# Sixteen score groups as float16 pairs with high halves cast on GpSimd, and five operand pairs and eleven stores issued later, in a fused attention and gated-layer kernel

## The chip, the cores and the metric

The program runs on one core of a Trainium2 chip, as one launch. The metric is the device time of that launch in microseconds. The kernel before took 1107.22 us (median of three runs, 1106.39 to 1107.66).

In what follows TensorE is PE (its weight loads are PEld), VectorE is DVE, ScalarE is ACT, GpSimd is POOL, and SyncE, which issues nearly all DMAs, is SP.

## The reference, cut to what matters

```python
def _attn_ref(q, k, v):                      # 8 batches, 12 heads, 448 positions, head size 64
    scores = (1 / sqrt(64)) * np.matmul(q, k.transpose(0, 1, 3, 2)) - np.log(448)
    attn = 1.0 / (1.0 + np.exp(-scores))     # a sigmoid, no softmax
    return np.matmul(attn, v)

def _moe_ref(x, w_gate, w_val, w_out):       # x: 3584 tokens x 768; hidden size 1536
    gate = 1.0 / (1.0 + np.exp(-(x @ w_gate)))
    val = x @ w_val
    return gate * val @ w_out
```

The attention output, with its heads side by side, is the `x` of the second function. The weights come as float64 and are turned into float32 on the chip.

## The kernel before, in words

**Two parts.** The first part computes the attention and, beside it, prepares operands. The second part computes the gated layer in visits: four pairs of batches, each visited twice for the first layer (`visits` of kind A, parts 0 and 1) and once for the output layer (kind C). A product of two matrices there is done with seven half-size products (Strassen's way, `N_OPS = 7`), each operand of which is a pair of float16 matrices, a high half and a low half. Every matmul of the second part has 128 x 128 weights and 448 columns.

**The attention loop.** It runs over 24 groups `m` (8 batches times 3 groups of four heads) and 7 blocks `g` of keys: 168 beats. In a beat PE computes the scores of `(m, g)` (`scores`, line 541), then the product with the values for the block two beats earlier (`values`, line 576); ACT turns the scores into sigmoids (line 568) and copies finished outputs (line 593). The scores come in two forms. In float32, PE issues 4 matmuls straight from the loaded queries and keys (`qk`). In the split form a group has been turned into float16 pairs beforehand, and PE issues 12 matmuls for a beat: low times high, high times low, high times high. `in_halves(m)` says which form a group has: the odd groups from 3 on, and the even ones listed in `ALSO` (line 37: 14, 18, 22), 14 groups in all. Beats of a group in float32 are called f32 beats below, the others f16 beats.

**How a group is split (`split_qk`, line 508).** It is a generator in three steps. Two groups ahead (at `g = 0` of `m - 2`), DVE takes the largest absolute value of each row (lines 514 and 516). At `g = 4` of `m - 2`, four tiny matmuls are queued behind the next beat's scores, which bring the largest of all rows to every row (`qk_sums`, line 559; ACT copies it out, line 570). One group ahead (at `g = 0` of `m - 1`), DVE makes a power of two from it (lines 522 and 523), casts the scaled group into the high half (line 527, twice 128 x 896), subtracts to get the low half (line 529, twice 128 x 896), and computes the factor that ACT undoes the scale with (lines 531 and 532). The halves of odd groups lie in tiles `hl`, those of even groups in the tiles `b0` and `b1`. The scores of `(m, 0)` need all of this.

**What else runs in the loop.** The weights are converted (`convert`), one step in some of the beats: ACT and DVE put float32 words together (lines 213, 214, 224, 227), POOL clamps (line 207), DVE adds (line 272), POOL casts high halves (`whl`, line 390), DVE subtracts low halves (line 242), SP stores them. No step is made in beats `g = 0, 1` when the next group is in halves. From `m = 8` on the first pair of batches is loaded back as `x` (`load_x`), summed on DVE (`subtract_x`, line 358), and split into its 21 operands (`split_x`, line 420): for each, POOL casts the high half (line 390) and, one step later, DVE subtracts the low half (line 401). A step is made at `g = 2` and `g = 5` from `m = 12` on, so all 24 steps fall into the loop. Each two operands share a tile `b`; SP stores it to `b_dram` (line 427) so that it can be loaded again for the second visit of that pair, much later. The eighteen source tiles take their names in turn from `SUMS` and from `xt0` to `xt5`; `xt` tiles live in the pool of the attention part alone, those of `SUMS` longer.

**The visits.** A `Visit` runs the seven products of a unit, two units interleaved, one product (9 matmuls) and one `tick` at a time. Its operands are `self.b`; the first visit's products take operands in the order 0, 1, 2, 4, 3, 5, 6 (`ORDER`). Weight operands come through a ring of 8 tiles `A` that SP fills in program order. In each of the first four visits the next pair's `x` is loaded, summed on POOL and split by ACT and DVE (from tick 29 or 33 on), and stored.

**What sets the order.** Each engine runs its own instructions in the order in which the code issues them, and waits at semaphores. A few instructions that stand first on an engine behind the change from the first part to the second are put further ahead, to where their inputs are ready. SP's DMAs are issued in program order.

Of the kernel before, what the change touches and what calls it, by code (L numbers as in the profile page):

```python
# [15 lines left out]
ALU = mybir.AluOpType  # L16
# [19 lines left out]

ALSO = 14, 18, 22

# [13 lines left out]
JPS_OF_PARTS = (range(0, 4), range(4, 6))  # L52
# [9 lines left out]
def sigmoid_attention_glu_kernel(ctx: ExitStack, tc: tile.TileContext, qk, v, wg, wv, wo, out):  # L62

    nc = tc.nc
# [7 lines left out]
    KC = KT // 2  # L72
# [5 lines left out]
    N_OPS = 7  # L78
# [267 lines left out]
    xs, bs, new_bs = {}, {}, {}  # L346
# [42 lines left out]
    def scaled_gpsimd(to, x, s):  # L389
        nc.gpsimd.tensor_scalar(out=to, in0=x, scalar1=s, scalar2=1.0, op0=ALU.mult, op1=ALU.mult)  # L390
# [20 lines left out]
    def load_b(pr):  # L411

        for at in range(KEPT + 1):
# [4 lines left out]
            yield  # L418

    def split_x(pr, cast=scaled, engine=nc.gpsimd):  # L420

# [3 lines left out]
        for at in range(len(work) + 3):  # L425
            while unsent:
                nc.sync.dma_start(**unsent.pop(0))
            if at == len(work) + 2:
                yield
                break  # L430
# [63 lines left out]
    with tc.manual_schedule(), tc.tile_pool(name="att", bufs=2) as att, tc.tile_pool(name="sc", bufs=2, space=PSUM) as scp, \  # L494
# [10 lines left out]
        def in_halves(m):  # L505
            return 1 < m < B * NQ and (m % 2 == 1 or m in ALSO)

        def split_qk(m):
# [17 lines left out]
            for t in range(2):  # L526
                nc.vector.tensor_scalar(out=hl[0][:, t], in0=x[:, :, t], scalar1=s_[:, t:t + 1], scalar2=None, op0=ALU.mult)
            for t in range(2):
# [111 lines left out]
        first_x = 2 * NQ + 2  # L640
        tags = itertools.chain(SUMS, (f"xt{i}" for i in range(2 * KC)))

# [8 lines left out]
        for m in range(B * NQ):  # L651
            for g in range(7):
# [11 lines left out]
                if g == (m == 2) and in_halves(m + 1):  # L664
                    next(splitting[m + 1])
                if g == (5 if m == 1 else 4) and in_halves(m + 2):
                    next(splitting[m + 2])
# [13 lines left out]
                if m >= first_x + 2 and g in (2, 6):  # L681
                    next(x_sums, None)
                if m >= first_x + 4 and g in (2, 5):
                    next(splits, None)
# [9 lines left out]
        assert next(x_loads, None) is None and next(x_sums, None) is None  # L694
        for _ in splits:
            pass

# [181 lines left out]
    class Visit:  # L879


        def __init__(self, v_):
            (_, self.pr, part), nxt = visits[v_], visits[v_ + 1]
            self.v_, self.jps, self.b, self.keep = v_, JPS_OF_PARTS[part], dict(new_bs), nxt[0] == "C"
            self.p, self.ticks = 0, starts[v_ + 1] - starts[v_]
# [10 lines left out]
        def tick(self):  # L896
            self.p += 1
            p, left = self.p, self.ticks - self.p
            if p % 2 == 0 and self.early:
                self.early.pop(0)()  # L900
# [242 lines left out]
```

## Time and profile before

| | |
|---|---|
| median of three runs | 1107.22 us |
| the profiled execution, its own time | 1107.39 us |
| span of its instructions | 1105.7 us |
| granted TensorE clock | 1.00 |
| matmuls and weight loads on PE | 7738 each |
| busy: PE / DVE / ACT / POOL, whole span | 1100.1 / 770.2 / 672.1 / 423.4 us |
| `bd<-b` stores of operand pairs | 30 of 448 KB, 3 of 224 KB |

Times in the profile are microseconds from the first instruction. A row of groups reads: line, engine, operation, what it writes `<-` what it reads, partitions x elements, count, then busy time and the mean of one in ns, then the idle time of the engine just before. A row of the timeline reads: start, length, engine, line, operation. Rows with the same engine may overlap, since an engine takes up the next instruction before the last one's end is recorded. The chain of waits is followed back from the last instruction: at each step to what released it.

### The profile page before, as it was taken

The page shows a single profiled execution, that of the slowest core. Times are in us where ns is not written, and L with a number is a line of the kernel's source. Part 1 is how long each engine was busy: PE and PEld are TensorE (multiplying, and loading weights), DVE is VectorE, ACT ScalarE, POOL GpSimd, SP SyncE. Part 2 cuts the span into 40 slices and gives each one's busy share as a digit, 9 for nine tenths or more (in the row PEclk, how much of TensorE's full clock was granted, in tenths as well). Part 3 has the DMA queues.
Part 4 walks back from the last instruction along what each step waited for, and adds up shares of the span by engine and source line. Part 5 has one row for each costly group of instructions (what it writes and reads, how often), then busy time and mean ns, then how long its engine had stood idle before and what let it go on. Part 6 is the DMA issues. An engine that isn't in the chain of part 4 may idle for free.

```text
span 1105.7 us, 21560 instructions
## 1 busy us (share of the span) xinstructions
PE 1100.1 (99%) x7738; PEld 556.9 (50%) x7738; DVE 770.2 (70%) x1303; ACT 672.1 (61%) x1273; POOL 423.4 (38%) x398
## 2 busy tenths in 40 slices
PE   9999999999999999999999999999999999999998
PEld 3444454455555555555555555555555555555554
DVE  4998999977964474555667766674349687776863
ACT  5888888877576675765566767665545253243330
POOL 1132232243731351432334433242365293672940
PEclk9999999999999999999999999999999999999999
DMA  8899888689898467733766899797856877868644
GB/s 320 275 297 349 282 276 284 233 269 366 268 304 279 152 216 219 258 105 93 225 204 203 267 360 302 216 313 199 241 155 198 262 217 216 274 201 247 187 124 142
DMA packets 174540, 265.35 MB, mean 240 GB/s; under 512 B 49249, under 2 KB 151265, under 8 KB 174433
## 3 DMA queue, kind: packets, MB, share of 16 engines
q1 hardware_dynamic: 174144, 263.60, 74.2%
q8 instruction: 60, 0.98, 0.4%
q14 instruction: 48, 0.39, 0.1%
q10 hardware_dynamic: 288, 0.38, 0.1%
HBM read 182.48 MB, written 81.43 MB: 239 GB/s over the span
## 4 chain that ended last, share of the span: by engine, by line
PE 99%; ACT 0%; DVE 0%; DVEq 0%; issue 0%
PE un L737 78%; PE av L583 12%; PE sc L553 10%; PE sc L618 0%; ACT a L568 0%; PE un L705 0%; DVE g L1023 0%; DVEq L1138 0%; PE sc L559 0%; PE sc L565 0%; DVE bias L85 0%; DVEq L1023 0%
## 5 line engine op out<-in xcount | busy, mean ns | idle before, releaser
L737 PEld LDWEIGHTS <-A 128*128 128x128 f16 x3024 | 295.5, 98 | 275.9 <-DMA ad<-whl 0.7
L737 PE MATMUL un<-b,A 128*128 128x448 f16 x1512 | 296.5, 352 | 0.0
L737 PE MATMUL un<-b,v 128*128 128x448 f16 x1512 | 296.4, 352 | 0.0
L737 PE MATMUL un<-hh,A 128*128 128x448 f16 x1008 | 272.9, 352 | 0.0
L737 PEld LDWEIGHTS <-v 128*128 128x128 f16 x1512 | 147.7, 98 | 137.5
L737 PE MATMUL un<-hl,A 128*128 128x448 f16 x504 | 177.6, 352 | 0.0
L583 PE MATMUL av<-a,v 64*64 64x448 f32 x1344 | 156.8, 538 | 0.0
L948 POOL TENSOR_TENSOR g<-c,g 128x448 f32<-128x448 f32 x44 | 59.7, 1357 | 173.9 <-DVE c L720 79.3
L207 POOL TENSOR_SCALAR wf<-wf 128x384 f32<-128x384 f32 x72 | 42.1, 585 | 203.2 <-ACT wf L230 120.4
L568 ACT ACTIVATE a<-sc,bias,qkb 128x896 f32<-128x896 f32 x98 | 108.1, 1104 | 12.7 <-PE sc L553 9.3
L720 DVE TENSOR_TENSOR c<-un,u 128x448 f32<-128x448 f32 x72 | 44.8, 623 | 94.5 <-PE un L737 84.0
L933 ACT ACTIVATE g<-c,back 128x448 f32<-128x448 f32 x72 | 48.1, 668 | 77.1 <-DVE c L720 76.4
L568 ACT ACTIVATE a<-sc,bias 128x896 f32<-128x896 f32 x70 | 70.4, 1007 | 30.0 <-PE sc L553 26.6
L358 POOL TENSOR_TENSOR v<-v 128x448 f32<-128x448 f32 x48 | 64.1, 1365 | 51.2 <-DVE hl L401 50.1
L358 POOL TENSOR_TENSOR b<-b 128x448 f32<-128x448 f32 x48 | 67.5, 1441 | 40.5 <-DVE hl L401 40.5
L583 PEld LDWEIGHTS av<-a,v 64*64 64x64 f32 x1344 | 49.3, 133 | 39.2 <-issue 29.6
L553 PE MATMUL sc<-qk 64*64 64x448 f32 x560 | 65.6, 540 | 0.4 <-ACT a L568 0.4
L753 ACT COPY p<-un 128x448 f32<-128x448 f32 x48 | 25.4, 528 | 58.4 <-PE un L737 58.3
L720 DVE TENSOR_TENSOR c<-un,p 128x448 f32<-128x448 f32 x48 | 29.8, 621 | 41.8 <-PE un L737 40.6
L553 PE MATMUL sc<-hl 64*64 64x448 f16 x924 | 57.5, 349 | 0.0
L358 POOL TENSOR_TENSOR r<-r 128x448 f32<-128x448 f32 x36 | 45.2, 1266 | 30.2 <-DVE b L401 29.9
L110 ACT ACTIVATE junk<-g 128x448 bf16<-128x448 f32 x88 | 50.5, 574 | 7.0 <-POOL g L948 6.0
(362 smaller groups left out, 1425.4 us busy)
## 6 DMA issues: line engine op xcount, KB each, us to landing
A<-ad SPq DMA_DIRECT2D x168, 192.0 KB, 3.3
A<-oo SPq DMA_DIRECT2D x168, 192.0 KB, 2.9
qk<-qk SPq DMA_DIRECT2D x23, 896.0 KB, 7.5
h<-g SPq DMA_DIRECT2D x88, 224.0 KB, 3.2
ad<-whl SPq DMA_DIRECT2D x84, 192.0 KB, 3.8
bd<-b SPq DMA_DIRECT2D x30, 448.0 KB, 3.4
b<-bd SPq DMA_DIRECT2D x30, 448.0 KB, 6.2
v<-vv SPq DMA_DIRECT2D x24, 448.0 KB, 4.9
```

The costliest lines, as they stand in the source:

```text
L110: nc.scalar.activation(junk[:, :x.shape[-1]], x, AF.Abs, accum_out=to)
L207: nc.gpsimd.tensor_scalar(out=f, in0=f, scalar1=F32_MAX, scalar2=F64_ZERO, op0=ALU.min, op1=ALU.max)
L358: engine.tensor_tensor(out=to, in0=x, in1=y, op=ALU.subtract)
L553: nc.tensor.matmul(sc[halves[p], h, :S], lhsT=ks_, rhs=qs, start=i == 0, stop=i == 2 or not in_halves(m))
L568: nc.scalar.activation(a, sc[:, :, :S], AF.Sigmoid, bias=bias, scale=unit)
L583: nc.tensor.matmul(avs[m][p][halves[h], :S], lhsT=vt[halves[p], g, h], rhs=a[halves[p], h], start=g == 0, stop=g == 6)
L720: engine.tensor_tensor(out=to, in0=x, in1=y, op=ALU.add)
L737: nc.tensor.matmul(acc, lhsT=w, rhs=m, start=begin and i == 0, stop=i == len(terms) - 1, skip_group_check=not begin)
L753: nc.scalar.copy(c, acc)
L933: nc.scalar.activation(gates[i], acc, AF.Sigmoid, scale=of_unit[0])
L948: nc.gpsimd.tensor_tensor(out=h, in0=acc, in1=gates[i], op=ALU.mult)
```

## The change

- `ALSO` becomes 10, 14, 18, 20, 22: groups 10 and 20 are split as well, 16 groups instead of 14.
- The high halves of these groups are cast by POOL (`scaled_gpsimd`, line 389) instead of DVE, and the step that held the casts and the subtractions is cut in two: the power of two and the casts stay at `g = 0` of the group before, the subtractions and the factor move to `g = 3` (`g = 1` and `g = 4` for group 3).
- The split of the first pair's operands begins three groups later (`m = 15`), so 18 of its 24 steps fall into the attention loop. The rest are made in the ticks of the first visit, whose products read `new_bs` as it fills up. `SUMS[:9]` and the `xt` tiles change places in part, so that the operands left over have their sources in tiles that outlive the loop.
- The eleven stores of the first pair's operand tiles are kept back (`kept_stores`) and issued in the second visit, one in every second tick.

```diff
-ALSO = 14, 18, 22
+ALSO = 10, 14, 18, 20, 22
...
+    kept_stores = []
+
     def split_x(pr, cast=scaled, engine=nc.gpsimd):
...
         for at in range(len(work) + 3):
-            while unsent:
+            while unsent and pr:
                 nc.sync.dma_start(**unsent.pop(0))
             if at == len(work) + 2:
+                kept_stores.extend(unsent)
                 yield
                 break
...
             hl = halves_of[m % 2]
             for t in range(2):
-                nc.vector.tensor_scalar(out=hl[0][:, t], in0=x[:, :, t], scalar1=s_[:, t:t + 1], scalar2=None, op0=ALU.mult)
+                scaled_gpsimd(hl[0][:, t], x[:, :, t], s_[:, t:t + 1])
+            yield
             for t in range(2):
                 nc.vector.scalar_tensor_tensor(out=hl[1][:, t], in0=x[:, :, t], scalar=s_[:, t:t + 1], in1=hl[0][:, t],
                                                op0=ALU.mult, op1=ALU.subtract)
...
-        tags = itertools.chain(SUMS, (f"xt{i}" for i in range(2 * KC)))
+        tags = itertools.chain(SUMS[:9], ("xt0", "xt1", "xt2", "xt3", "g1", "xt4", "g2", "xt5", "g3"))
...
                 if g == (m == 2) and in_halves(m + 1):
                     next(splitting[m + 1])
+                if g == 3 + (m == 2) and in_halves(m + 1):
+                    next(splitting[m + 1])
...
-                if m >= first_x + 4 and g in (2, 5):
+                if m >= first_x + 7 and g in (2, 5):
                     next(splits, None)
...
-        for _ in splits:
-            pass
...
-            self.v_, self.jps, self.b, self.keep = v_, JPS_OF_PARTS[part], dict(new_bs), nxt[0] == "C"
+            self.v_, self.jps, self.b, self.keep = v_, JPS_OF_PARTS[part], dict(new_bs) if v_ else new_bs, nxt[0] == "C"
...
             p, left = self.p, self.ticks - self.p
+            if self.v_ == 0:
+                next(splits, None)
+                if p == 2 * N_OPS:
+                    self.b = dict(new_bs)
+            if self.v_ == 1 and p % 2 == 0 and kept_stores:
+                nc.sync.dma_start(**kept_stores.pop(0))
```

Three places show what this does to the engines. The first is DVE around the split of the last group, 23, which is made while group 22 is computed (`qk_3800` and `qk_3927` are its maxima, `qk_3801` and `qk_3928` its powers of two). Before:

```order
L242 SCALAR_TENSOR_TENSOR whl<-wf,w20s,whl 128x384
L522 TENSOR_TENSOR qk_3800<-qka 128x2
L523 TENSOR_SCALAR qk_3801<-qk_3800 128x2
L527 TENSOR_SCALAR hl<-qk,qk_3801 128x896 x2
L529 SCALAR_TENSOR_TENSOR hl<-qk,qk_3801,hl 128x896 x2
L531 TENSOR_SCALAR qk_3802<-qk_3800 128x2
L532 TENSOR_SCALAR qkb<-qk_3802 128x1
```

And with the change:

```order
L525 TENSOR_TENSOR qk_3927<-qka 128x2
L526 TENSOR_SCALAR qk_3928<-qk_3927 128x2
L242 SCALAR_TENSOR_TENSOR whl<-wf,w20s,whl 128x384
L132 TENSOR_REDUCE w21m<-all 128x1
L126 TENSOR_SCALAR invw<-w21m 128x1
L127 TENSOR_SCALAR w21s<-invw 128x1
L128 TENSOR_SCALAR w21s<-w21s 128x1
L129 TENSOR_SCALAR invw<-invw 128x1
L401 SCALAR_TENSOR_TENSOR b<-g_1872,x0s,b 128x448
L358 TENSOR_TENSOR g_1872<-xt,g_1872 128x448
L533 SCALAR_TENSOR_TENSOR hl<-qk,qk_3928,hl 128x896 x2
L535 TENSOR_SCALAR qk_3929<-qk_3927 128x2
```

The two casts are gone from DVE, and eight instructions of the weights and of `x` now stand between the power of two and the subtractions.

The second place is POOL from there to the start of the first visit (`whl` are high halves of weights, `b<-u`, `b<-g` those of `x` operands; `L207 wf` is the first visit's weight conversion). Before:

```order
L390 TENSOR_SCALAR b<-xt,x0s 128x448
L390 TENSOR_SCALAR whl<-wf,w20s 128x384
L390 TENSOR_SCALAR whl<-wf,w21s 128x384
L390 TENSOR_SCALAR b<-xt,x0s 128x448
L390 TENSOR_SCALAR whl<-wf,w21s 128x384 x2
L390 TENSOR_SCALAR b<-xt,x0s 128x448
L390 TENSOR_SCALAR whl<-wf,w21s 128x384 x4
L207 TENSOR_SCALAR wf<-wf 128x384 x6
```

And with the change:

```order
L390 TENSOR_SCALAR whl<-wf,w20s 128x384
L390 TENSOR_SCALAR hl<-qk,qk_3928 128x896 x2
L390 TENSOR_SCALAR whl<-wf,w21s 128x384
L390 TENSOR_SCALAR b<-g_2154,x0s 128x448
L390 TENSOR_SCALAR whl<-wf,w21s 128x384 x2
L390 TENSOR_SCALAR b<-g_2384,x0s 128x448
L390 TENSOR_SCALAR b<-g_1872,x0s 128x448
L390 TENSOR_SCALAR b<-g_2154,x0s 128x448
L390 TENSOR_SCALAR whl<-wf,w21s 128x384 x4
L390 TENSOR_SCALAR b<-u_1571,x0s 128x448
L390 TENSOR_SCALAR b<-u_1584,x0s 128x448
L207 TENSOR_SCALAR wf<-wf 128x384
```

Group 23's casts stand in the queue behind a cast of weights, and most casts of `x` operands still stand ahead of the first visit's work.

The third place is DVE at the start of the first visit (`L720`, now `L724`, is its first sum out of PSUM). Before:

```order
L401 SCALAR_TENSOR_TENSOR b<-xt,x0s,b 128x448
L242 SCALAR_TENSOR_TENSOR whl<-wf,w21s,whl 128x384 x2
L720 TENSOR_TENSOR c_4257<-un,p_4204 128x448
L213 TENSOR_SCALAR wf<-wf 128x384
L214 SCALAR_TENSOR_TENSOR wf<-b,wf 128x384
```

And with the change:

```order
L242 SCALAR_TENSOR_TENSOR whl<-wf,w21s,whl 128x384 x2
L401 SCALAR_TENSOR_TENSOR b<-u_1571,x0s,b 128x448
L401 SCALAR_TENSOR_TENSOR b<-u_1584,x0s,b 128x448
L401 SCALAR_TENSOR_TENSOR b<-c_1641,x0s,b 128x448
L401 SCALAR_TENSOR_TENSOR b<-g_1872,x0s,b 128x448
L724 TENSOR_TENSOR c_4396<-un,p_4335 128x448
L401 SCALAR_TENSOR_TENSOR b<-g_2154,x0s,b 128x448
L213 TENSOR_SCALAR wf<-wf 128x384
L214 SCALAR_TENSOR_TENSOR wf<-b,wf 128x384
L401 SCALAR_TENSOR_TENSOR b<-g_2384,x0s,b 128x448
```

The last five subtractions of `x` operands stand in the first visit: three ahead of its first sum and two behind it.

## The prediction, made before the changed kernel ran

> **What bounds the kernel now.** I read the profile from the whole to the part: the page's busy times and chain of waits, the busy times by stage, then the chain in order of time inside the attention part.
>
> ```profile
> PE 1100.1 (99%) x7738; PEld 556.9 (50%) x7738; DVE 770.2 (70%) x1303; ACT 672.1 (61%) x1273; POOL 423.4 (38%) x398
> PE 99%; ACT 0%; DVE 0%; DVEq 0%; issue 0%
> core 0: us, PE busy (x) PEld busy (x) DVE busy (x) ACT busy (x) POOL busy (x), PEclk, DMA share, GB/s
> 0.00:242.42 242.42, 241.07 (x3188) 112.36 (x3188) 215.05 (x424) 197.42 (x236) 67.54 (x92) 1.00 0.84 286
> 242.42:1101.44 859.02, 859.02 (x4554) 444.54 (x4550) 554.31 (x878) 474.64 (x1037) 355.89 (x306) 1.00 0.72 228
> 36.00:242.00 206.00, 195.39 (x382) 1.00 0.83 282
> ```
>
> The first window is the attention part, the second the visits up to the last matmul. PE is busy through all 859.02 us of the visits and, but for 1.35 us at the start, through the attention part; the chain that ended last is PE alone. So only PE's own work can shorten the kernel, and anything that makes PE wait lengthens it one for one. The last row (DVE alone, from 36 us on) is the warning: beside PE, DVE has 206.00 - 195.39 = 10.6 us left. DVE makes the float16 halves that PE needs.
>
> What a beat costs on PE is read from the chain in order of time (start, length, what):
>
> ```profile
> 203.34 0.75 PE av L583 x8
> 204.09 0.75 PE sc L553 x8
> ...
> 209.36 0.75 PE av L583 x8
> ...
> 213.74 0.75 PE av L583 x8
> 214.49 0.57 PE sc L553 x12
> ...
> 219.02 0.75 PE av L583 x8
> ...
> 220.32 0.02 PE sc L559 x3
> 220.34 0.81 PE av L583 x8
> ```
>
> From 203.34 to 209.36 lie four f32 beats: 6.02 us, 1.505 each. From 213.74 to 219.02 lie four f16 beats: 5.28 us, 1.320 each. The twelve float16 matmuls take 0.57 where the four float32 ones (x8 with their loads) take 0.75; the values take 0.75 in both.
>
> **The change, part by part.** *Two more groups in halves* (10 and 20). Fourteen beats fall by 1.505 - 1.320 = 0.185: 2.59 us. Each split group also brings one set of tiny matmuls (L559), which lengthens its beat by 0.06 (the values behind it stand at 0.81, not 0.75): 2 x 0.06 = 0.12. Net **-2.47 us**, all on PE, and so on the end, if nothing new waits.
>
> ACT follows PE through these beats. An f16 beat costs it a little more, but it still waits for PE where f16 groups follow each other:
>
> ```profile
> 224.51 1.10 ACT L568 ACTIVATE a<-sc,bias,qkb 128x896 f32<-128x896 f32 x1 [0.23 <-PE sc L553]
> ```
>
> That row is from group 22, inside the run 21 to 23, where ACT has every copy of two f16 groups behind it and is still ahead. A longer run (17 to 23) has the same load per group, so I cost it at nothing; were the 0.23 not there, each further f16 group would cost its excess over PE, some tenths.
>
> *The casts on POOL.* The rows of DVE's part and of POOL's casts:
>
> ```profile
> L514 DVE TENSOR_REDUCE qkm<-qk 128x2 f32<-128x1792 f32 x14 | 28.1, 2006 | 0.0
> L529 DVE SCALAR_TENSOR_TENSOR hl<-qk,qk,hl 128x896 f16<-128x896 f32 x22 | 24.9, 1171 | 0.0
> L527 DVE TENSOR_SCALAR hl<-qk,qk 128x896 f16<-128x896 f32 x22 | 16.0, 769 | 1.1
> L527 DVE TENSOR_SCALAR b<-qk,qk 128x896 f16<-128x896 f32 x6 | 3.8, 683 | 0.1
> L401 DVE SCALAR_TENSOR_TENSOR b<-xt,x0s,b 128x448 f16<-128x448 f32 x9 | 6.6, 744 | 0.0
> L390 POOL TENSOR_SCALAR whl<-wf,w11s x7: 581/887/1409, 153.3 to 192.5; 128x384 f16<-128x384 f32 x7
> L390 POOL TENSOR_SCALAR b<-xt,x0s x9: 632/996/1320, 172.0 to 235.2; 128x448 f16<-128x448 f32 x9
> L390 POOL TENSOR_SCALAR b<-p,x0s x2: 997/1192/1387, 133.0 to 134.8; 128x448 f16<-128x448 f32 x2
> L529 DVE SCALAR_TENSOR_TENSOR hl<-qk,qk,hl x22: 1131/1144/1467, 29.0 to 228.8; 128x896 f16<-128x896 f32 x22
> ```
>
> DVE loses 16.0 + 3.8 = 19.8 us of casts. It gains two groups: reduction 2.0, two subtractions 2.3, five small ones like L523 (0.17, its row below), 0.9, so 2 x 5.2 = 10.4. Five subtractions for `x` (L401, 0.74) leave the loop: 3.7. Net DVE has 13.1 us less to do.
>
> The trace has no 128 x 896 cast on POOL. From below, it can't beat the 0.63 of the 448-column one alone; from above, it is twice the longest one, 2 x 1.39 = 2.77. Undisturbed casts grow from 581 (384 columns) to 632 (448), 0.8 ns a column, which gives 632 + 448 x 0.8 = 0.99 us. I take **1.0**. DVE's price for running beside POOL is bounded by its own row: a subtraction that takes 1.131 alone took at most 1.467, so 0 to 0.34 for each of 32 casts, 0 to 10.8 us. Even the upper end leaves DVE with less work than before.
>
> *The subtractions three beats later.* This step decides. For the two groups with the least room before (DVE first, then the PE row that needs the result; between them the means of what now stands in between at group 23):
>
> ```profile
> 178.42 0.17 DVE L523 TENSOR_SCALAR qk<-qk 128x2 uint32<-128x2 uint32 x1
> 178.62 1.28 DVE L527 TENSOR_SCALAR b<-qk,qk 128x896 f16<-128x896 f32 x2
> 179.82 2.21 DVE L529 SCALAR_TENSOR_TENSOR b<-qk,qk,b 128x896 f16<-128x896 f32 x2
> 183.83 0.75 PE L553 MATMUL sc<-b 64*64 64x448 f16 x12
> L242 DVE SCALAR_TENSOR_TENSOR whl<-wf,w20s,whl 128x384 f16<-128x384 f32 x7 | 4.6, 654 | 0.0
> L358 DVE TENSOR_TENSOR xt<-g,xt 128x448 f32<-128x448 f32 x4 | 2.8, 689 | 0.1
> L132 DVE TENSOR_REDUCE w20m<-all 128x1 f32<-128x128 f32 x1 | 0.3, 277 | 0.0
> L129 DVE TENSOR_SCALAR invw<-invw 128x1 f32<-128x1 f32 x6 | 0.9, 144 | 0.0
> ...
> 225.82 0.42 DVE L523 TENSOR_SCALAR qk<-qk 128x2 uint32<-128x2 uint32 x1
> 227.76 2.20 DVE L529 SCALAR_TENSOR_TENSOR hl<-qk,qk,hl 128x896 f16<-128x896 f32 x2
> 231.58 0.75 PE L553 MATMUL sc<-hl 64*64 64x448 f16 x12
> ```
>
> Group 18 had 183.83 - 182.03 = 1.80 us to spare. After: casts start at 178.6 and end at 180.6, the second subtraction ends 1.14 later, near 181.8, so 2.0 to spare. POOL has to be late by more than that, or a cast to last 2.04 us ((183.83 - 1.14 - 178.6) / 2), before PE waits. Group 23 had 231.58 - 229.96 = 1.6. After, eight instructions stand between (the order rows): L242 0.65, L132 0.28, four tiny ones of 0.15, L401 0.74, L358 0.69, together 3.0 us; DVE reaches the subtractions near 226.2 + 3.0 = 229.2 and ends them near 231.4, 0.2 before PE needs them. But DVE comes there earlier by what it no longer does: two casts like group 18's (1.28) for group 22 alone. So about 1.5. I cost the step at nothing. Its bounds are 0 and, with casts of 2.77, 183.83 overrun by 178.6 + 5.54 + 1.14 - 183.83 = 1.5 us per tight group.
>
> Queued behind a waiting subtraction are DVE's weight steps and, behind those, SP's stores of weights; nobody needs them before the visits.
>
> *Five operands in the first visit.* Order rows show POOL's casts mostly still in the loop, and DVE's subtractions at the visit's start. Both engines stood idle there:
>
> ```profile
> 247.16 0.51 POOL L207 TENSOR_SCALAR wf<-wf 128x384 f32<-128x384 f32 x1 [5.81 <-ACT wf L230]
> 249.52 0.62 DVE L720 TENSOR_TENSOR c<-un,p 128x448 f32<-128x448 f32 x1 [6.64 <-PE un L737]
> ```
>
> Three subtractions of 0.8 fit into DVE's 6.64. The first product that reads them is the sixth, five products of 9 matmuls (859.02 / 4554 = 0.189 each, 1.70 a product) after 242.42, so at 250.9; they are ready near 246 even with 1 us of DVE's backlog. Cost nothing; without that idle time it would be at most the 3.7 us of all five.
>
> *The stores in the second visit.* They leave SP's queue and the transfers of the loop (a small help), and come back between 340 and 376 us:
>
> ```profile
> 340.00:376.00 36.00, 36.00 (x192) 18.65 (x191) 15.32 (x27) 24.39 (x64) 10.66 (x12) 1.00 0.76 255
> A<-ad SPq DMA_DIRECT2D x14, 192.0 KB, 4.2
> GB/s 320 275 297 349 282 276 284 233 269 366 268 304 279 152 216 219 258 105 93 225 204 203 267 360 302 216 313 199 241 155 198 262 217 216 274 201 247 187 124 142
> ```
>
> Ten of 448 KB and one of 224 KB are 4.8 MB, 134 GB/s over these 36 us on top of 255: 389, where the page's busiest slice has 366. The excess is 23 x 36 us, 0.8 MB, some 2 us of lateness. Weight operands land 4.2 us after issue, in a ring of eight, each worth 1.70 or more: 13.6 us of cover against 6.2. Cost nothing; bounds 0 and 2.
>
> **The sum.** The profiled execution took 1107.39 (span 1105.7, 1.69 around it), 0.17 above the median. 1107.39 - 2.47 = 1104.92; against the median, 1107.22 - 2.47 = **1104.8**.
>
> **The rivals.** *Low halves late.* The subtraction waits for POOL, which is held up by the cast queued ahead, or DVE brings a backlog. For: 0.2 us at group 23 without DVE's relief, casts at up to 1.39 for half the columns. Against: 1.8 and more elsewhere. Price: one to four groups late by 0.3 to 1.5, say 0.3 to 3 us in all: 1105.1 to 1107.8, no change that counts.
>
> *POOL takes DVE's time away.* If each of 32 casts stopped DVE for its whole 1.0, DVE would lose 32 us against 10.6 + 13.1 = 23.7 of room; the missing 8.3 come out of PE: 1107.22 - 2.47 + 8.3 = **1113.0, slower**. It decides from 23.7 / 32 = 0.74 us per cast. Against it: the row of L529 has at most 0.34, and POOL's own cast is stretched too (632 to 1320), so the two share the delay. The Trainium skill (SBUF — State Buffer, section "SBUF: two separate sides") states this rule: GpSimd and a VectorE instruction with two SBUF inputs take one port pair in turn, and the loser fully blocks. By it the sum would be this rival's; the stretched rows agree that there is a turn to wait for, not that every cast costs its length.
>
> *The second visit's transfers hold PE up*, by up to 2 us: 1106.8.
>
> **How the numbers follow.** Forecast 0.64, late halves 0.22, POOL's price 0.10, the transfers 0.04. A measurement of this kernel can tell 0.2%, or 2.2 us, from no change; the forecast lies only 0.26 us beyond that line, so of its 0.64 I give 0.55 to faster and 0.09 to the same; of late halves 0.04 and 0.18; the transfers' 0.04 to the same; of POOL's price, which may come in part, 0.08 to slower and 0.02 to the same. That is 0.59, 0.33 and 0.08. Range: from 1104.2 (0.6 below, the spread of the three runs) to 1107.0, which takes in most of the late halves and leaves out their end and the slower rival.
>
> **What would show it right or wrong.** Right: the first matmul of the visits starts 2.5 us earlier than 242.42, the visits last 859.0 as before, groups 10 and 20 have beats of 1.32, POOL casts of 896 columns take about 1.0, and each low half ends before its group's first scores. Wrong: a wait of PE's on the subtraction (now L533) at a group's first beat; DVE subtractions well over 1.47; a gap in PE's row near 251 or between 340 and 380.

## The result, and the profile after

| | before | with the change |
|---|---|---|
| median | 1107.08 us (1106.39 to 1107.66, four runs) | 1114.16 us (1113.97 to 1114.23, four runs) |
| ratio | | 1.0064, 95% interval 1.0047 to 1.0081 |
| the profiled execution, its span | 1107.39, 1105.7 us | 1113.97, 1112.3 us |

The change makes the kernel 0.64% slower, where 0.2% faster was forecast. The page of the changed kernel, its busy times and the chain that ended last:

```profile
PE 1099.8 (99%) x7802; PEld 554.3 (50%) x7802; DVE 779.7 (70%) x1291; ACT 673.6 (61%) x1275; POOL 481.8 (43%) x430
PE 90%; DVE 8%; POOL 1%; ACT 0%; issue 0%; DMA 0%; DVEq 0%; SPq 0%; POOLq 0%; ACTq 0%
```

The chain was PE alone before; now 8% of it is DVE. The next rows say in which stage. They are the busy times by stretch of the changed kernel: the attention part, the visits, then a stretch near the end of the loop (window, length, PE, PEld, DVE, ACT, POOL, granted clock, DMA share, GB/s).

```profile
0.00:249.00 249.00, 240.78 (x3252) 109.77 (x3252) 221.11 (x407) 198.67 (x238) 124.65 (x123) 0.99 0.78 265
249.00:1107.67 858.67, 858.67 (x4554) 444.54 (x4550) 557.75 (x883) 474.91 (x1037) 357.10 (x307) 1.00 0.73 232
...
237.10:240.51 3.41, 3.41 (x32) 1.35 (x28) 3.38 (x6) 1.69 (x2) 2.81 (x3) 0.50 0.59 181
```

The visits take 858.67 us, all of them PE, as before (859.02). The attention part ends at 249.00 instead of 242.42, 6.6 us later. PE stands idle in it for 8.2 us (before 1.35), and its busy time fell by 0.3 instead of 2.47. The third row tells most of it: from 237.10 to 240.51 PE had half its clock (the column before the last two), so that the same work took longer. Away from the waits the beats show the gain that was forecast. PE's timeline around the first scores of groups 21, 22 and 23 (start, length; in brackets the idle time before and what ended it):

```profile
213.86 0.76 PE L557 MATMUL sc<-hl 64*64 64x448 f16 x12 [2.04 <-DVE hl L533]
214.45 0.92 PE L587 MATMUL av<-a,v 64*64 64x448 f32 x8
...
215.77 0.92 PE L587 MATMUL av<-a,v 64*64 64x448 f32 x8
...
224.80 0.76 PE L557 MATMUL sc<-b 64*64 64x448 f16 x12 [1.40 <-DVE b L533]
...
236.45 0.76 PE L557 MATMUL sc<-hl 64*64 64x448 f16 x12 [2.22 <-DVE hl L533]
237.04 1.65 PE L587 MATMUL av<-a,v 64*64 64x448 f32 x8
238.47 1.34 PE L557 MATMUL sc<-hl 64*64 64x448 f16 x12
...
240.80 0.74 PE L557 MATMUL sc<-hl 64*64 64x448 f16 x12
```

A beat of a split group lasts 215.77 - 214.45 = 1.32, as forecast. But PE waits 2.04 us for group 21's low half, 1.40 for group 22's and 2.22 for group 23's, and behind the last wait two beats take 240.80 - 236.45 = 4.35 us instead of 2.64. All of PE's waits for low halves in the loop (us in total, times, the longest):

```profile
PE sc L557 <- DVE hl L533: 5.0, 3, 2.2
PE sc L557 <- DVE b L533: 1.9, 3, 1.4
```

The beats that hold such a wait are the last ones of groups 13 (0.39 us too long), 18 (0.92), 19 (0.43), 20 (2.21), 21 (1.63) and 22 (2.39): 8.0 us, and 1.7 of slow beats behind the last. That is 9.7, less the 2.5 that the shorter beats gain: 7.2. (The loop's first beats ran 0.7 us sooner in this execution, which makes it 6.5, against the 6.6 that were measured.)

What DVE and POOL did is in the groups of the attention part (out, in, shapes, count, busy, mean ns of one, idle before):

```profile
L533 DVE SCALAR_TENSOR_TENSOR hl<-qk,qk,hl 128x896 f16<-128x896 f32 x22 | 32.6, 1518 | 1.7 <-POOL hl L390 1.7
L517 DVE TENSOR_REDUCE qkm<-qk 128x2 f32<-128x1792 f32 x16 | 32.1, 2008 | 0.0
L533 DVE SCALAR_TENSOR_TENSOR b<-qk,qk,b 128x896 f16<-128x896 f32 x10 | 15.6, 1597 | 2.7 <-POOL b L390 2.7
L390 POOL TENSOR_SCALAR hl<-qk,qk 128x896 f16<-128x896 f32 x22 | 27.6, 1266 | 32.3 <-DVE qk L526 28.7 <-PE sc L557 3.5
```

A subtraction took 1.15 to 1.17 on average before and takes 1.52 to 1.60 now. Little of the idle time ahead of it is waiting for POOL (1.7 and 2.7 us in all): the casts mostly come in time, and the subtractions are slow. Together the 32 take 12.1 us more than at their means of before. DVE alone from 36 us to the end of the attention part, after and then before:

```profile
36.00:249.00 213.00, 201.76 (x365) 0.99 0.77 256
```

```profile
36.00:242.42 206.42, 195.81 (x383) 1.00 0.83 282
```

DVE was to have 13.1 us less to do and had 5.95 more: 19 us came back, 12.1 of them in the subtractions, the rest spread over its other instructions.

### The profile page after: what moved, and what is told of

The parts are those of the page before. It is cut to its first block, busy times and chain, and to the rows that moved or that the text cites. A ratio compares the mean times of both kernels' runs of the same rounds, so it can differ in the third digit from the quotient of the medians.

```text
span 1112.3 us, 21725 instructions
## 1 busy us (share of the span) xinstructions
PE 1099.8 (99%) x7802; PEld 554.3 (50%) x7802; DVE 779.7 (70%) x1291; ACT 673.6 (61%) x1275; POOL 481.8 (43%) x430
## 4 chain that ended last, share of the span: by engine, by line
PE 90%; DVE 8%; POOL 1%; ACT 0%; issue 0%; DMA 0%; DVEq 0%; SPq 0%; POOLq 0%; ACTq 0%
PE un L741 77%; PE av L587 6%; PE sc L557 6%; DVE qkm L517 1%; DVE b L533 1%; DVE hl L533 1%; DVE whl L242 1%; DVE b L401 1%; DVE wf L272 1%; POOL b L390 0%; PE sc L622 0%; ACT a L572 0%; DVE wf L214 0%; DVE g L358 0%; POOL hl L390 0%
## 5 line engine op out<-in xcount | busy, mean ns | idle before, releaser
L572 ACT ACTIVATE a<-sc,bias,qkb 128x896 f32<-128x896 f32 x112 | 123.5, 1104 | 24.2 <-PE sc L557 14.1
L207 POOL TENSOR_SCALAR wf<-wf 128x384 f32<-128x384 f32 x72 | 48.3, 672 | 158.9 <-ACT wf L230 101.6
L724 DVE TENSOR_TENSOR c<-un,u 128x448 f32<-128x448 f32 x72 | 44.8, 622 | 94.0 <-PE un L741 83.5
L358 POOL TENSOR_TENSOR v<-v 128x448 f32<-128x448 f32 x48 | 64.1, 1364 | 51.2 <-DVE hl L401 50.2
L358 POOL TENSOR_TENSOR b<-b 128x448 f32<-128x448 f32 x48 | 67.6, 1443 | 40.6 <-DVE hl L401 40.6
L572 ACT ACTIVATE a<-sc,bias 128x896 f32<-128x896 f32 x56 | 56.3, 1007 | 23.9 <-PE sc L557 20.7
L358 POOL TENSOR_TENSOR r<-r 128x448 f32<-128x448 f32 x36 | 45.3, 1269 | 30.2 <-DVE b L401 29.9
L724 DVE TENSOR_TENSOR c<-un,p 128x448 f32<-128x448 f32 x48 | 29.8, 621 | 38.9 <-PE un L741 37.4
L557 PEld LDWEIGHTS <-hl 64*64 64x64 f16 x924 | 28.3, 108 | 49.0 <-issue 34.4
```

The source lines that it names most:

```text
L207: nc.gpsimd.tensor_scalar(out=f, in0=f, scalar1=F32_MAX, scalar2=F64_ZERO, op0=ALU.min, op1=ALU.max)
L358: engine.tensor_tensor(out=to, in0=x, in1=y, op=ALU.subtract)
L557: nc.tensor.matmul(sc[halves[p], h, :S], lhsT=ks_, rhs=qs, start=i == 0, stop=i == 2 or not in_halves(m))
L572: nc.scalar.activation(a, sc[:, :, :S], AF.Sigmoid, bias=bias, scale=unit)
L724: engine.tensor_tensor(out=to, in0=x, in1=y, op=ALU.add)
```

## The experiments

Each variant was timed beside the kernel before, and the ratio is to that. The expectations speak of four theories: 1, a cast on POOL takes DVE's time; 2, the subtractions stand too late, whoever casts; 3, DVE has too much to do with two more groups; 4, the steps of `x` that are moved crowd the last groups.

| kernel | median us | ratio, 95% interval |
|---|---|---|
| e4: before, list of five groups | 1115.26 | 1.0072 [1.0057, 1.0087] |
| e12: before, edits to `x` | 1107.07 | 0.9999 [0.9989, 1.0008] |
| e9: before, both | 1107.03 | 1.0003 [0.9994, 1.0012] |
| e1: e9 with the step cut | 1111.98 | 1.0043 [1.0029, 1.0058] |
| the change: e1 with casts on POOL | 1114.16 | 1.0064 [1.0047, 1.0081] |
| e10: e9 with casts on POOL, not cut | 1122.81 | 1.0138 [1.0124, 1.0152] |
| e2: the change with 14 groups | 1106.94 | 0.9999 [0.9990, 1.0008] |
| e3: the change without the edits to `x` | 1117.36 | 1.0093 [1.0078, 1.0108] |
| e8: before, every cast made on both engines | 1125.17 | 1.0163 [1.0149, 1.0176] |
| e17: e1 cut at `g = 2` | 1106.76 | 0.9998 [0.9989, 1.0008] |
| e15: the change, weight steps moved | 1118.84 | 1.0107 [1.0092, 1.0122] |
| e16: e1, weights spread longer | 1107.49 | 1.0001 [0.9992, 1.0011] |
| e14: the change, weights spread longer | 1109.45 | 1.0021 [1.0011, 1.0031] |
| e13: e9, weights spread longer | 1104.93 | 0.9978 [0.9969, 0.9987] |
| e5, e6, e11: other lists | below | below |

### The change taken apart

**The list alone (e4).** Two more groups in the kernel before.

```diff
-ALSO = 14, 18, 22
+ALSO = 10, 14, 18, 20, 22
```

> The kernel before with the list of five and nothing else: casts on DVE, step not cut, x steps as before. If two more groups (10.4 us of DVE) fit into DVE's 10.6 us of room without a wait: 1104.6 to 1105.2. Theory 3: PE waits, 1108 to 1112.

1115.26. The list alone loses 8.2 us, more than the whole change: 10.4 us more work for a DVE that had 10.6 idle, and the attention part ends at 249.21.

**The edits to `x` alone (e12).** The changed kernel with the old list, the casts on DVE and the step in one piece.

```diff
-ALSO = 10, 14, 18, 20, 22
+ALSO = 14, 18, 22
...
-                scaled_gpsimd(hl[0][:, t], x[:, :, t], s_[:, t:t + 1])
-            yield
+                nc.vector.tensor_scalar(out=hl[0][:, t], in0=x[:, :, t], scalar1=s_[:, t:t + 1], scalar2=None, op0=ALU.mult)
...
-                if g == 3 + (m == 2) and in_halves(m + 1):
-                    next(splitting[m + 1])
```

> The x edits alone: list of three, casts on DVE, step not cut. PE's work is as before and had no waits: 1106.7 to 1107.3, the attention part ends at 242.4, DVE is busy some 3.7 us less, and neither the first nor the second visit shows a wait of PE. If the stores in the second visit or the operands in the first cost anything: above 1107.5.

The time is unchanged. DVE alone, from 36 us to the end of the attention part, and the visits:

```profile
36.00:242.45 206.45, 193.14 (x375) 1.00 0.78 262
```

```profile
242.45:1101.40 858.95, 858.95 (x4554) 444.53 (x4550) 558.57 (x885) 475.19 (x1037) 358.13 (x307) 1.00 0.73 232
```

DVE has 195.81 - 193.14 = 2.7 us less (3.7 were forecast), and PE is busy through the visits without a gap. The two steps on the first and the second visit stand.

**Both (e9).** e12 with the list of five.

```diff
-ALSO = 14, 18, 22
+ALSO = 10, 14, 18, 20, 22
```

> The changed kernel with casts on DVE and the step not cut: list of five and x edits. Against the run with casts on DVE and the step cut (1111.98) it tells what the cut does. Theory 2 (subtractions three beats later come too late): 1108 to 1110. If the cut makes no difference and DVE's load decides: 1111 to 1113.

1107.03: the edits to `x`, worth nothing alone, take back all 8.2 us that the list costs. What is left is one long wait of PE's at the end of group 21, and it is not for a low half:

```profile
PE sc L568 <- DVE each L122: 1.7, 1, 1.7
```

`each` is a step of the weights. A few tiny matmuls on it stand in PE's own queue, so a late DVE stops PE there too. (Two of the expectations below call this halves that came 2.0 us late at group 22; the trace has that low half ready at 219.53, before PE's wait ends at 221.30.)

**The step cut in two, casts still on DVE (e1).** The changed kernel with one line undone.

```diff
-                scaled_gpsimd(hl[0][:, t], x[:, :, t], s_[:, t:t + 1])
+                nc.vector.tensor_scalar(out=hl[0][:, t], in0=x[:, :, t], scalar1=s_[:, t:t + 1], scalar2=None, op0=ALU.mult)
```

> The changed kernel with the high halves of the score groups cast by DVE again; the five-entry list, the cut step and the x edits stay. Theory 1 (a POOL cast takes DVE's time: subtractions went from 1.14 to 1.57 us): the waits of PE go, the attention part ends near 240 to 241 us, 1104.8 to 1106. Theory 2 (the subtractions stand too late, whoever casts): PE waits as long as with the change, 1112 or more. Theory 3 (DVE has too much to do with two more groups): 32 casts of 0.7 are 22 us more on DVE, so worse than the change, 1116 or more.

1111.98. In this order of steps the cut costs 4.95 us against e9, and POOL's casts the last 2.2 of the change; e10 below shows that another order gives other shares. PE's longest waits and its timeline at group 23:

```profile
PE sc L557 <- DVE hl L533: 3.6, 2, 3.0
```

```profile
234.67 1.33 PE L557 MATMUL sc<-hl 64*64 64x448 f16 x12 [2.95 <-DVE hl L533]
235.79 1.70 PE L587 MATMUL av<-a,v 64*64 64x448 f32 x8
```

About 1.5 of the 4.95 are slow beats behind that wait, as in the changed kernel.

**The change without the edits to `x` (e3).**

```diff
-                if m >= first_x + 7 and g in (2, 5):
+                if m >= first_x + 4 and g in (2, 5):
...
-            if self.v_ == 0:
-                next(splits, None)
```

(The stores go back as well.)

> The changed kernel with all x edits undone: 24 split steps from group 12 on, stores in the loop. Theory 4 (moving the x steps into groups 15 to 23 crowds the last groups): 1105 to 1109. Theories 1 to 3: five more subtractions in the loop, 3.7 us more on DVE, 1115 to 1119.

1117.36: the edits are worth 3.2 us in the changed kernel, within the range of theories 1 to 3. Theory 4 is out.

### What POOL's casts cost DVE

**Casts on POOL, not cut (e10).** The subtractions stand right behind the casts.

```diff
                 scaled_gpsimd(hl[0][:, t], x[:, :, t], s_[:, t:t + 1])
-            yield
             for t in range(2):
...
-                if g == 3 + (m == 2) and in_halves(m + 1):
-                    next(splitting[m + 1])
```

> The changed kernel with the step not cut: POOL casts, and DVE's subtractions stand directly behind the power of two, at g = 0 of the group before. It completes the square of (DVE or POOL) x (cut or not): 1107.03, 1111.98 and 1114.16 are known. If the place of the subtractions and POOL's price add up: 1107.0 + 2.2 = 1109.2. If DVE mainly loses by standing still until POOL has cast (1.0 us a group against 1.3 of casts saved) and the subtractions, now beside less of POOL's other work, keep their 1.14: 1106 to 1108. If POOL's price grows when the queue ahead of the cast holds DVE up: 1112 or more.

1122.81. DVE and POOL around group 21's split (timelines of the two engines):

```profile
219.12 3.28 DVE L532 SCALAR_TENSOR_TENSOR hl<-qk,qk,hl 128x896 f16<-128x896 f32 x2 [1.30 <-POOL hl L390]
```

```profile
218.07 2.00 POOL L390 TENSOR_SCALAR hl<-qk,qk 128x896 f16<-128x896 f32 x2 [1.58 <-DVE qk L526]
220.05 1.42 POOL L390 TENSOR_SCALAR whl<-wf,w20s 128x384 f16<-128x384 f32 x1
```

The first subtraction by itself, and the row of the subtractions by line (shortest, median and longest, ns):

```profile
219.12 1.89 DVE L532 SCALAR_TENSOR_TENSOR hl<-qk,qk,hl 128x896 f16<-128x896 f32 x1 [1.30 <-POOL hl L390]
L532 DVE SCALAR_TENSOR_TENSOR hl<-qk,qk,hl x22: 1140/1680/1897, 28.5 to 244.3; 128x896 f16<-128x896 f32 x22
```

This is the cleanest measurement of the case. A cast of 896 columns takes 1.00 on POOL, the value that was estimated. Beside it the pair of subtractions takes 3.28 where it took 2.21: 1.07 us lost, and 1.30 of waiting before it. DVE saved two casts, 1.28 us, and paid 2.37. The POOL cast that runs beside the first subtraction is not lengthened at all; the cast of weights behind it is (1.42, where the shortest of its size in the kernel before took 0.58).

e9, e1, e10 and the change make a square, and its two parts don't add up. Not cut, POOL's casts cost 1122.81 - 1107.03 = 15.8 us; cut, 2.2. With the casts on DVE the cut costs 4.95; with POOL's it gains 1122.81 - 1114.16 = 8.65. What stands between casts and subtractions is a delay when DVE casts, and covers the wait for POOL when POOL does: ahead of the subtractions DVE waits 20.6 us for POOL's casts in e10 and 4.4 in the change.

**The change with 14 groups (e2).** The list of before, everything else as changed.

```diff
-ALSO = 10, 14, 18, 20, 22
+ALSO = 14, 18, 22
```

> The changed kernel with the list of three (14, 18, 22), so 14 groups in halves, cast on POOL, subtractions three beats later, x edits in place. Theory 1: 28 of 32 casts still disturb DVE, 1109 to 1113. Theory 2: the late subtractions stay, 1109 to 1113. Theory 3: the load is gone, 1107 or a little above.

1106.94, and no late group. DVE alone, from 36 us to the end of the attention part:

```profile
36.00:241.74 205.74, 189.21 (x347) 1.00 0.78 262
```

Against e12 (193.14) the casts moved and the step is cut, which moves no work off DVE or onto it. DVE gained 3.9 us where its 28 casts had taken 19.8. So 15.9 came back, 0.57 us per cast.

**Every cast made on both engines (e8).** The kernel before; POOL makes each cast a second time into a tile that nothing reads. DVE's program is unchanged.

```diff
+                scaled_gpsimd(junk_of_casts, x[:, :, t], s_[:, t:t + 1])
```

> The kernel before with every high half cast twice: on DVE as before, and on POOL into a tile that nobody reads. DVE's own program is unchanged, so what it takes longer is POOL's price. Theory 1 (0.5 to 0.6 us of DVE a cast): DVE is busy 14 to 17 us longer than 196.3 after 36 us, more than its room of 10, and PE waits: 1109 to 1114. The prediction's bound (at most 0.34 a cast): at most 9.5 us longer, 1107 to 1108.

1125.17. The groups on DVE, and DVE alone from 36 us to the end of the attention part:

```profile
L531 DVE SCALAR_TENSOR_TENSOR hl<-qk,qk,hl 128x896 f16<-128x896 f32 x22 | 35.0, 1628 | 0.0
L514 DVE TENSOR_REDUCE qkm<-qk 128x2 f32<-128x1792 f32 x14 | 28.1, 2007 | 0.0
L528 DVE TENSOR_SCALAR hl<-qk,qk 128x896 f16<-128x896 f32 x22 | 22.1, 1046 | 1.1
```

```profile
36.00:259.63 223.63, 217.31 (x382) 0.97 0.77 261
```

The same program on DVE takes 217.31 instead of 195.81: 21.5 us for 28 casts, 0.77 each. The casts on DVE suffer too (769 to 1046 ns), the reduction doesn't (2006 and 2007).

### Why the cut costs 4.95, and what the rest is

**No weight step ahead (e15).** The changed kernel; the weight steps that stand between casts and subtractions at `g = 2` are held back.

```diff
-                if done < min(n_weights, due_at(beat) - 1e-6) and not (g < 2 and in_halves(m + 1)):
+                if done < min(n_weights, due_at(beat) - 1e-6) and not (g < 3 and in_halves(m + 1)):
```

> The changed kernel with no weight step in beat g = 2 either when the next group is in halves, so that none stands between the power of two and the subtractions on DVE. If the cut costs because weight steps now stand ahead of the subtractions (1 to 2 us each): the halves come that much earlier, 1107 to 1111. If the steps, made up for later in the group, crowd DVE all the same or POOL's casts end last anyway: 1113 to 1116.

A miss: 1118.84, 4.7 worse. No more than three rows are left between casts and subtractions, and DVE now reaches the subtractions before POOL has cast. Its wait for the `hl` casts, 1.7 us in the changed kernel:

```profile
DVE hl L533 <- POOL hl L390: 12.1, 10, 1.8
```

That is e10's loss again in part. Whether the weight steps, with one beat fewer to be made in, also crowd the beats that are left was not tested. As a test of what the cut costs it was spoilt by the casts being on POOL.

**Cut at `g = 2` (e17).** The same question with the weight steps left alone: e1, the subtractions one beat earlier.

```diff
-                if g == 3 + (m == 2) and in_halves(m + 1):
+                if g == 2 + (m == 2) and in_halves(m + 1):
```

> The changed kernel with its casts back on DVE, and the subtractions at g = 2 of the group before instead of g = 3. No weight step is made at g = 0 and 1 there, so on DVE nothing stands between casts and subtractions in 13 of 16 groups, and the subtractions stand one beat's steps further ahead than with g = 3. If the cut's 4.95 us are what stands ahead of the subtractions (2 to 12 instructions in the kernel with g = 3), they go: 1107.0 to 1108.0, with group 14 and 22 late as in the uncut kernel. If they come from somewhere else (the change's other code, the place of the factor, POOL), it stays near 1112.

1106.76: the cut's 4.95 us are gone. The order on DVE at group 22's split, with `g = 3` (e1):

```
L530 TENSOR_SCALAR b<-qk,qk_3733 128x896 x2
L242 SCALAR_TENSOR_TENSOR whl<-wf,w20s,whl 128x384
L272 TENSOR_TENSOR wf<-wf 128x384
L132 TENSOR_REDUCE w21m<-w21c 128x1
L122 TENSOR_SCALAR each<-w21m 128x128
L401 SCALAR_TENSOR_TENSOR b<-xt,x0s,b 128x448
L533 SCALAR_TENSOR_TENSOR b<-qk,qk_3733,b 128x896 x2
```

With `g = 2` (e17) the subtractions and the factor follow the casts at once, and the five rows come behind them. Over all groups one to twelve rows stand between casts and subtractions with `g = 3`, one or none with `g = 2`. So with the casts on DVE the cut costs what it lets in ahead of the subtractions. (Casts on POOL with `g = 2` were not timed.)

**The weights spread longer (e13, e16, e14).** One number: the beat by which all weight steps are due. Later means less work for DVE per beat at the end of the loop. The edit was made to e9, to e1 and to the changed kernel.

```diff
-PACE = (0, 0), (20, 0.25), (50, 0.57), (90, 0.76), (146, 1)
+PACE = (0, 0), (20, 0.25), (50, 0.57), (90, 0.76), (151, 1)
```

> List of five (with 20) and x edits, casts on DVE, step not cut, and the last weights converted some beats later (the pace's last point 151 in place of 146), so that DVE has less to do at groups 18 to 22 and more behind. If the load at that place makes group 22 late: the 2.0 us go, 1104.8 to 1105.8. If not: 1107, and if the weights come too late for the first visit, more.

> The changed kernel with its casts back on DVE (the step stays cut, subtractions three beats later) and the weight conversion's last point at beat 151 instead of 146. If the cut costs only where the end of the loop is crowded, the 4.95 us between 1107.03 and 1111.98 go with the crowding: 1105.0 to 1106.5, waits before low halves under 1.5 us in all, and the 1109.45 of the kernel with casts on POOL and the weights later is then POOL's own price of 3 us or more. If the cut has a price of its own wherever it stands (a subtraction three beats later is three beats less of cover), it stays: 1104.93 + 4.95 = 1109.9, and POOL costs nothing beyond it.

> The changed kernel as it is (POOL casts, step cut, list of five, x edits) with the pace's last point at 151 in place of 146, which alone took 2.1 us off the kernel with DVE casts and the step not cut. If the changed kernel's late halves come from too little room on DVE at groups 19 to 23 alone: most of its 9 us of waits go, 1105 to 1107. If POOL's price, spread over all groups from 13 on, is the larger part: it gains 2 to 4 us, 1110 to 1112.

e13 takes 1104.93, ratio 0.9978 [0.9969, 0.9987], the fastest of all. Its attention part:

```profile
0.00:239.86 239.86, 238.51 (x3252) 109.83 (x3253) 216.55 (x430) 198.54 (x238) 61.38 (x86) 1.00 0.79 269
```

PE is idle for 1.35 us, as before, and busy for 238.51 instead of 241.07: 2.56 less, against the 2.47 of the prediction. With the casts on DVE and the step whole, the two groups give just what PE's arithmetic says.

With the cut it is 1107.49 (e16), with POOL's casts too 1109.45 (e14). So where the end of the loop is less crowded the cut costs 2.6 and POOL 2.0; neither theory that was written for e16 (0 or all 4.95) holds. No slow beats follow a wait in either, while e1 had 1.5 us of them.

### Other lists

All with the edits to `x`, casts on DVE and the step whole (as e9).

```diff
-ALSO = 10, 14, 18, 20, 22
+ALSO = 10, 14, 18, 22
```

> The x edits and group 10 (list 10, 14, 18, 22), casts on DVE, step not cut. Theory 3 says that the second new group, 20, in the crowded end, does the harm: DVE has 3.7 us less for x and 5.2 more, lags at groups 8 to 10 were below zero; no wait of PE, 1.23 us less than before: 1105.6 to 1106.2. If any further group overfills DVE: 1107.5 or more.

```diff
-ALSO = 10, 14, 18, 20, 22
+ALSO = 4, 10, 14, 18, 22
```

> As e5, with group 4 in halves as well (list 4, 10, 14, 18, 22); group 4 is prepared in the first 40 us, where DVE was busy for about half of the time. If room on DVE at the place decides: two groups gained, 2.47 us less than before, 1104.4 to 1105.0. If the sum over the whole loop decides: as bad as with groups 10 and 20, 1110 or more.

```diff
-ALSO = 10, 14, 18, 20, 22
+ALSO = 10, 14, 16, 18, 22
```

> List of five with 16 in place of 20 (10, 14, 16, 18, 22), x edits, casts on DVE, step not cut. In the run with 20 DVE's halves came 2.0 us late at group 22 and 0.24 late at 14, while groups 17 to 19 had 4 to 7 us to spare. If room at the place decides: no late group but 14, 1104.6 to 1105.4. If the sum over the loop decides: 1107 as with 20.

1106.21 (0.9990 [0.9981, 0.9999]), 1110.59 (1.0034 [1.0021, 1.0046]) and 1109.06 (1.0016 [1.0007, 1.0025]). The last two are misses: I had looked for room where groups 4 and 16 stand, and PE waits showed up elsewhere: with group 4 one of 1.6 us at 64.65 us and one of 1.4 before group 14, with group 16 one of 1.1 before group 16 itself and one of 1.45 before group 18. How much DVE has idle over a stretch does not tell whether a group there will be late.

## Why the prediction was wrong, point by point

**Two more groups in halves.** Right: beats of 1.32, and 2.56 us less of PE in e13. ACT, costed at nothing, has 0% of the chain. (A slip that changes nothing: the rows marked x8 are eight matmuls, their loads not among them, for four that the code issues.)

**The casts on POOL.** Wrong, and this is the first step that failed: "Net DVE has 13.1 us less to do", and "0 to 0.34 for each of 32 casts". The cast's own time was right (1.0 estimated, 1.00 in e10). The price was read from the row of L529 of the kernel before, longest one 1467. But there POOL only ran casts of 384 and 448 columns, and only two of its 28 subtractions had any of POOL's work beside them, the pair whose second took the 1467 (DVE's row, then POOL's, of the kernel before):

```profile
69.96 2.85 DVE L529 SCALAR_TENSOR_TENSOR hl<-qk,qk,hl 128x896 f16<-128x896 f32 x2
69.65 2.23 POOL L390 TENSOR_SCALAR whl<-wf,w01s 128x384 f16<-128x384 f32 x2
```

A longest one seen by chance is no upper bound for an overlap that the change makes the rule. Measured: 0.57 us per cast in e2, 0.77 in e8, up to 0.75 on a single subtraction (1.89 in the changed kernel and in e10, 1.14 alone). A cast on DVE is worth 0.71 (19.8 / 28). Nothing to speak of is left, and with 10.4 us of two more groups DVE ends with more to do, not less.

**The subtractions three beats later.** Wrong, the second step: "I cost the step at nothing", with 1.5 us to spare at group 23, because DVE would come there earlier. It came later. DVE's timeline of the changed kernel there, and then POOL's:

```profile
229.41 0.43 DVE L526 TENSOR_SCALAR qk<-qk 128x2 uint32<-128x2 uint32 x1
229.74 0.63 DVE L242 SCALAR_TENSOR_TENSOR whl<-wf,w20s,whl 128x384 f16<-128x384 f32 x1
...
231.12 1.09 DVE L401 SCALAR_TENSOR_TENSOR b<-g,x0s,b 128x448 f16<-128x448 f32 x1
232.24 1.32 DVE L358 TENSOR_TENSOR g<-xt,g 128x448 f32<-128x448 f32 x1
233.48 2.91 DVE L533 SCALAR_TENSOR_TENSOR hl<-qk,qk,hl 128x896 f16<-128x896 f32 x2
```

```profile
229.79 0.96 POOL L390 TENSOR_SCALAR whl<-wf,w20s 128x384 f16<-128x384 f32 x1
230.72 2.36 POOL L390 TENSOR_SCALAR hl<-qk,qk 128x896 f16<-128x896 f32 x2
```

The eight instructions in between were named rightly and priced at 3.0 us; they take 233.48 - 229.74 = 3.7, since L401 and L358 run beside POOL's casts (1.09 and 1.32 for 0.74 and 0.69). The pair takes 2.91 for 2.21. From the power of two to the last low half it is 7.0 us where the prediction had 5.6 (225.82 to 231.4). And the power of two itself comes at 229.41, 4.6 us after group 22's first scores at 224.80, at which it stands in the code. Before, it came 3.5 us after them (225.82 against this row):

```profile
222.34 0.75 PE L553 MATMUL sc<-b 64*64 64x448 f16 x12
```

So DVE came 1.1 us later where the prediction had it 1.3 earlier. The 1.5 to spare, less 2.4 and less 1.4, make 2.3 us late, and PE's wait was 2.22. With that lag a step written three beats later in the code runs more than six beats (8.7 us) behind group 22's first scores.

Group 18, the other one that the prediction looked at, was not the worst place: the largest waits sit before groups 21 to 23. The room of 10.6 us on DVE was a sum over 206 us. From 185 us on, DVE had 57.42 - 55.28 = 2.1 of it before, and 2.7 of 64 with the change:

```profile
185.00:242.42 57.42, 57.42 (x832) 28.23 (x824) 55.28 (x99) 49.60 (x59) 22.88 (x26) 1.00 0.74 242
```

```profile
185.00:249.00 64.00, 57.34 (x844) 26.14 (x836) 61.26 (x99) 49.05 (x59) 46.77 (x41) 0.97 0.60 186
```

So the forecast's 1104.8 needed more than the casts back on DVE and the step whole: e9, with both, still takes 1107.03, and only the thinner end of the loop in e13 brings it.

**One microsecond of waiting is one microsecond.** "Anything that makes PE wait lengthens it one for one" was too low: the last wait of 2.22 was followed by 1.7 us of slow beats.

**Five operands in the first visit, the stores in the second.** Right: no gap in PE's visits (858.67 us; e12 the same), DVE relieved by 2.7.

**The rivals.** The slower one had the time nearly right, 1113.0 against 1114.16, and the engine that loses: in e10 the first subtraction (219.12) starts just behind POOL's second cast (218.07 + 1.00), overlaps the 0.95 us of it that are left (to 220.07), and loses 0.75 (1.89 for 1.14). The Trainium skill's rule of the exclusive lock (SBUF — State Buffer, section "SBUF: two separate sides") would have it lose all 0.95; the trace comes within 0.2 of that, and agrees that the cast which started first is not lengthened. What was not right is the way to the sum. Averaged over the run the price is 0.57, below the 0.74 from which the rival was to decide: the median subtraction of the changed kernel takes 1.47 (`hl`) or 1.52 (`b`), not 1.89. DVE is not full over the whole loop (201.76 of 213.00); it is late where it has no room, at the end. "Low halves late" was the wait that was seen, but it was priced at one to four groups of 0.3 to 1.5, and it was six of up to 2.4.

**What stays open.** Why the edits to `x` and the later weights interact so strongly with the list (0 alone, 8.2 with five groups) is explained only in kind: a DVE with no reserve passes every delay on to the next group. No run shows the course of it step by step.

## What to carry to other kernels

Work moved from VectorE to GpSimd beside two-input subtractions gave back most of what it saved here: measure that with the extra work on GpSimd and VectorE's program unchanged, and do not take the longest instruction that happens to be in the trace as the bound. Before a step is put later, read on its engine both what will stand ahead of it and how far the engine already lags behind the one that needs it; three beats in the code were six on the chip. Room on an engine is read stage by stage, not as a sum. And where an engine has no reserve in one stretch, thin out that stretch first: here one number in the pace of the weights brought what the change was after.

## What the runs showed of the hardware

**Waits can cost PE its clock.** In the changed kernel the granted clock is 0.50 from 237.10 to 240.51 (a row further above), which costs PE 1.7 us. PE had been idle for 2.22 of the 3.41 us just before. The same stretch of the changed kernel, and then two of e17 that follow each other:

```profile
233.69:237.10 3.41, 1.19 (x24) 0.46 (x20) 3.38 (x5) 1.00 (x1) 3.41 (x4) 1.00 0.62 231
```

```profile
215.66:219.07 3.41, 2.84 (x48) 1.14 (x40) 3.30 (x6) 2.50 (x4) 0.00 (x0) 1.00 0.31 114
219.07:222.49 3.42, 1.87 (x32) 0.96 (x36) 3.38 (x9) 1.45 (x3) 0.62 (x1) 1.00 0.34 125
```

In e17 PE waits 2.11 us and the clock stays whole: the wait lies across two stretches, with 0.57 and 1.55 idle. The other traces agree. In the loops of seven of the 18 kernels the clock falls to 0.50, 13 times in all, for 3.41 us or twice that; within a trace these falls and the clock's first rise to 1.00 lie whole multiples of 3.41 us apart. Each stretch of 3.41 us before one holds 2.0 to 3.4 us of idle time, and no other stretch at full clock holds more than 1.8. So what counts here is how the wait falls on a grid of such stretches, not its length alone.

The Trainium skill (TensorE: Matmul & The Clock Gate, section "What's actually happening") has a clock of half rate after an idle window of about 3.4 us that runs freely. The length, the half rate and the free run agree with these traces; but the window need not be idle throughout, 2.0 us of it were enough.

**POOL slows DVE by the kind of instruction.** Beside POOL's casts a subtraction with two inputs goes from 1.14 to as much as 1.89, a cast with one input from 0.77 to 1.05 on average (e8), and the reduction over 1792 columns stays at 2.01 in every run. A cast of 896 columns takes POOL 1.0 us where it is not held up (e10).
